# A three-stage kernel in fp32 products on one core: a weight quad's splits and sums spread over its products in the second MoE

## The chip, the cores and the metric

The kernel runs on one core of one Trainium2 chip. The metric is the time of one execution on the device in microseconds (us), here the median of three runs. The core has five engines with a queue of instructions each, which they work off in order: PE (TensorE, matrix products into PSUM), DVE (VectorE), ACT (ScalarE), POOL (GpSimd) and SP, which here only issues DMA transfers. An engine that waits for another's result holds everything behind it in its own queue.

## The reference

Three stages follow each other on 2304 tokens of width 512: a linear attention, a first MoE layer and a second one. Only the second MoE is touched:

```python
def _moe2_ref(x, domain_probs, w1, w2) -> np.ndarray:
    N, D = x.shape                                  # 2304, 512
    E = w1.shape[0]                                 # 4 experts, w1: 4 x 512 x 1024, w2: 4 x 1024 x 512
    p = domain_probs / (domain_probs.sum(-1, keepdims=True) + 1e-09)
    out = np.zeros((N, D), dtype=np.float32)
    for e in range(E):
        h = np.maximum(x @ w1[e], 0.0)
        out += p[:, e:e + 1] * (h @ w2[e])
    return out.astype(np.float32)
```

All experts are computed for all tokens. The result must be good to about fp32, so each factor of a product is split into a rounded high part and the remainder, its low part, and a product is three matmuls (`split3`, line 357: high by high, high by low, low by high).

## The kernel before

The attention and the first MoE (lines 1 to 880, the first 697 us) are recorded into a planner that sets the order of their instructions from costs and due times. The second MoE is written out by hand, in the order in which its instructions stand in the code: 3 passes over 768 tokens each, and in each pass 16 **quads**. A quad is a block of 256 hidden columns of one expert; the program goes through 48 of them (`for q in range(NALL)`, here numbered 0 to 47).

**Layer 1 of a quad** is a fast 2x2 block product: seven products of 384 tokens by 128 columns (`product(1)` to `product(7)`, 6 matmuls each) in place of eight. Their PSUM results are combined on DVE by `plus` (line 975) in a chain of four buffers `cp, cu, cv, cw` (tiles `xc`); ACT copies the first product to `cp` (line 977). Four results of the chain are hidden blocks: `hidden` lets ACT write the high part (relu, line 971) and DVE the low part (line 972). The seven products go through six PSUM banks (`l1b`), so PE can run most of a quad ahead of DVE.

**Layer 2** runs one pair of quads behind: in quad q the pair n2 = q // 2 - 1 is summed over for three blocks of 128 tokens, the **token sums** `l2(0)`, `l2(1)`, `l2(2)` (`layer2`, 12 matmuls of 512 columns each). They alternate between two banks (`l2b`), which DVE empties into the accumulators `yacc` (line 929 the first time in a pass, line 931 later). So `l2(2)` can't begin until DVE has emptied `l2(0)`. PE's order in a quad is product 1, 2, `l2(0)`, product 6, 7, `l2(1)`, product 5, 4, `l2(2)`, product 3. On PE the operands tell them apart: products 1, 2, 6, 7, 5, 4, 3 read `xo0, xo1, xo4, xo5, xo3, xo2, xo6`, and token sums read hidden tiles `h00h` and so on.

**Preparing weights.** Two kinds of weights come through a ring of three staging buffers `raw` (512 KB a load), issued by `load_next` on SP in the fixed order w2 of quad 0, w2 of 1, w1 of 2, w2 of 2, w1 of 3, ... (line 903 issues w1, line 905 w2).
- `w1_steps(q + 1)`, a list `todo` of twelve steps in quad q for the next quad's layer 1: steps 0 to 3 are the sums and differences of weight blocks on DVE (line 800, into two buffers `wtmp`, each of two halves), steps 4 to 7 the high parts on ACT (line 802), steps 8 to 11 the low parts on POOL (line 804). Steps 4, 5, 8 and 9 read `raw` itself, the others the sums.
- `todo2`, the split of the quad's own w2, two halves: ACT high, POOL low (line 948). The token sums of the quad behind an odd one need it first.

**Where they stand before**: `prep(4)` issues the four sums right behind the first `hidden`, ahead of DVE's emptying of `l2(0)`; the ACT steps and the POOL steps come in pairs between later products; `todo2` stands at the end of the quad, and behind it two `load_next`, of which the first brings the w1 that the next quad's `prep(4)` needs. A load's transfer waits until the readers of its staging buffer have finished.

**Special quads.** Behind quads 3 and 19 `x_load` issues eight transfers of the next pass's tokens on SP (line 845), and four differences of them on DVE (`x_diff`, line 851) wait for these. In quads 15 and 31 (`xnew`) ACT and DVE or POOL split the next pass's seven operands (`x_hi`, `x_lo`, lines 859 and 863). In quad 47 there are no w1 steps. Behind it six token sums of the last pair follow.

Of the kernel before, what the change touches and what calls it, by code (L numbers as in the profile page):

```python
# [178 lines left out]
def attention_moe_moe_kernel(  # L179
# [17 lines left out]
    E, _, F2 = w1.shape  # L197
# [25 lines left out]
    def f32(ap):  # L223
        return ap.bitcast(F32)
# [127 lines left out]
    def split3(ps, pairs, start, stop):  # L352
        n = 0
        for (lh, ll), (rh, rl) in pairs:
            for a, b in ((lh, rh), (lh, rl), (ll, rh)):
                n += 1
                PE.matmul(ps, lhsT=a, rhs=b, start=start and n == 1, stop=stop and n == 3 * len(pairs))  # L357
# [414 lines left out]
    def w1_src(q):  # L772
        e, c = divmod(q % NQ, QPE)
        return w1[e, :, c * 256:(c + 1) * 256].rearrange("(k p) f -> p k f", p=128)

    def w2_src(q):
        e, c = divmod(q % NQ, QPE)
        return w2[e, c * 256:(c + 1) * 256, :].rearrange("(c p) d -> p c d", p=128)

    def w1_set(q):  # L780

        return [slots[2 * (q % 2) + i].rearrange(FULL)[:, 0:7 * 256].rearrange("p (o k f) -> p o k f", o=7, k=2) for i in range(2)]

    def w2_set(q):
        t = slots[4 + q % 4]
        return t[:, 0:2], t[:, 2:4]

    def w1_steps(q, raw, ta, tb):
        r = raw.bitcast(F32).rearrange("p (k f) -> p k f", k=4)
        s12, s34 = (f32(t).rearrange("p (o k f) -> p o k f", o=2, k=2) for t in (ta, tb))  # L790
        a11, a12, a21, a22 = r[:, 0:2, 0:128], r[:, 2:4, 0:128], r[:, 0:2, 128:256], r[:, 2:4, 128:256]
        wh, wl = w1_set(q)
        parts = [
            (wh[:, 0:2].rearrange("p o k f -> p (o k) f"), wl[:, 0:2].rearrange("p o k f -> p (o k) f"), r[:, :, 0:128], 512),
            (wh[:, 2], wl[:, 2], a22, 256),
            (wh[:, 3:5].rearrange("p o k f -> p (o k f)"), wl[:, 3:5].rearrange("p o k f -> p (o k f)"), s12.rearrange("p o k f -> p (o k f)"), 512),
            (wh[:, 5:7].rearrange("p o k f -> p (o k f)"), wl[:, 5:7].rearrange("p o k f -> p (o k f)"), s34.rearrange("p o k f -> p (o k f)"), 512),
        ]
        sums = [(s12[:, 0], a21, a22, ALU.add), (s12[:, 1], s12[:, 0], a11, ALU.subtract), (s34[:, 0], a11, a21, ALU.subtract), (s34[:, 1], a12, s12[:, 1], ALU.subtract)]
        steps = [("DVE", 0.36, lambda o=o, a=a, b=b, op=op: DVE.tensor_tensor(out=o, in0=a, in1=b, op=op)) for o, a, b, op in sums]  # L800
        for h, _, src, n in parts:
            steps.append(("ACT", c_act(n), lambda h=h, src=src: ACT.activation(out=h, in_=src, func=ACTF.Copy)))  # L802
        for h, l, src, n in parts:
            steps.append(("POOL", c_pool(n), lambda h=h, l=l, src=src: POOL.tensor_tensor(out=l, in0=src, in1=f32(h), op=ALU.subtract)))  # L804
        return steps
# [36 lines left out]
    def x_load(ps, kh):  # L842
        st = x_tiles()
        for h, o, j, i, n in x_pieces(ps):
            SP.dma_start(out=st["q"][2 * kh + h][:, :, o:o + n], in_=x2f[j][:, 2 * kh:2 * kh + 2, i:i + n])

    def x_diff(i):
        st = x_tiles()
        (b11, b12, b21, b22), (d2, d3, d4) = st["q"], st["t"]
        o, a, b = ((d3, b22, b12), (b12, b12, b11), (d2, b22, b12), (d4, b21, d2))[i]  # L850
        DVE.tensor_tensor(out=o, in0=a, in1=b, op=ALU.subtract)
# [6 lines left out]
    def x_hi(o):  # L858
        ACT.activation(out=x_tiles()["op"][o][0], in_=x_src(o), func=ACTF.Copy)

    def x_lo(o, eng):
        xh, xl = x_tiles()["op"][o]
        eng.tensor_tensor(out=xl, in0=x_src(o), in1=f32(xh), op=ALU.subtract)
# [34 lines left out]
    def load_next():  # L898
        if want:
            layer, q = want.pop(0)  # L900
            t = raw_ring.take().t
            if layer == 1:
                SP.dma_start(out=t.bitcast(F32).rearrange("p (k f) -> p k f", k=4), in_=w1_src(q))
            else:
                SP.dma_start(out=t.bitcast(F32).rearrange("p (c d) -> p c d", c=2), in_=w2_src(q))
            loads[layer, q] = t

    for _ in range(2):
        load_next()

    def hbuf(q, f, t):

        return hid[t][(2 * q + f) % len(hid[t])]

    def layer2(n, t):

        ps, pc = divmod(n, NQ // 2)
        e = 2 * pc // QPE
        y = l2b[(n * TP + t) % 2]
        half, sl = t // (TP // 2), slice(t % (TP // 2) * 128, (t % (TP // 2) + 1) * 128)  # L920
        for i in range(4):
            q, f = 2 * n + i // 2, i % 2
            hh, hl = hbuf(q, f, half)
            vh, vl = w2_set(q)
            split3(y, [((hh[:, sl], hl[:, sl]), (vh[:, f], vl[:, f]))], i == 0, i == 3)
        tt = ps * TP + t
        pe = pr[:, tt, e:e + 1]
        if pc == 0:
            DVE.tensor_scalar(out=acc[t], in0=y, scalar1=pe, scalar2=None, op0=ALU.mult)
        else:  # L930
            DVE.scalar_tensor_tensor(out=acc[t], in0=y, scalar=pe, in1=acc[t], op0=ALU.mult, op1=ALU.add)  # L931
        if pc == NQ // 2 - 1:
            SP.dma_start(out=out[tt * 128:(tt + 1) * 128, :], in_=acc[t])
# [6 lines left out]
    for q in range(NALL):  # L940
        ps, qi = divmod(q, NQ)
        wh, wl = w1_set(q)
        n2 = q // 2 - 1
        todo = []
        if 2 <= q + 1 < NALL:
            todo = [fn for _, _, fn in w1_steps(q + 1, loads.pop((1, q + 1)), tmp_ring.take().t, tmp_ring.take().t)]
        r2, (vh, vl) = loads.pop((2, q)).bitcast(F32).rearrange("p (c d) -> p c d", c=2), w2_set(q)
        todo2 = [lambda c=c: (ACT.activation(out=vh[:, c], in_=r2[:, c], func=ACTF.Copy), POOL.tensor_tensor(out=vl[:, c], in0=r2[:, c], in1=f32(vh[:, c]), op=ALU.subtract)) for c in range(2)]  # L948
        xnew = qi == NQ - 1 and ps + 1 < NPASS

        def product(p):
            o, x = PROD[p]
            bk = l1b[nprod[0] % len(l1b)][:, 0:NH]
            nprod[0] += 1
            split3(bk, [((wh[:, o, k], wl[:, o, k]), (xop[x][0][:, k], xop[x][1][:, k])) for k in range(2)], True, True)
            if xnew:
                x_hi(x)
                x_lo(x, POOL if p in (2, 7, 4) else DVE)
            return bk

        def prep(n):
            for _ in range(min(n, len(todo))):
                todo.pop(0)()

        def l2(i):
            if n2 >= 0:
                layer2(n2, 3 * (q % 2) + i)

        def hidden(f, t, src):
            hh, hl = hbuf(q, f, t)  # L970
            ACT.activation(out=hh, in_=src, func=ACTF.Relu)
            DVE.scalar_tensor_tensor(out=hl, in0=src, scalar=0.0, in1=f32(hh), op0=ALU.max, op1=ALU.subtract)

        def plus(o, bk, a):
            DVE.tensor_tensor(out=o, in0=bk, in1=a, op=ALU.add)  # L975

        ACT.activation(out=cp, in_=product(1), func=ACTF.Copy)  # L977
        p2 = product(2)
        plus(cw, p2, cp)
        hidden(0, 0, cw)  # L980
        prep(4)
        l2(0)
        plus(cu, product(6), cp)
        prep(2)
        plus(cv, product(7), cu)
        prep(2)
        l2(1)
        p5 = product(5)
        plus(cw, p5, cv)
        hidden(1, 1, cw)  # L990
        plus(cu, p5, cu)
        prep(2)
        plus(cv, product(4), cv)
        hidden(1, 0, cv)
        prep(2)
        l2(2)
        plus(cu, product(3), cu)
        hidden(0, 1, cu)
        for fn in todo2:
            fn()  # L1000
        load_next()
        load_next()
        if qi == 3 and ps + 1 < NPASS:
            for kh in range(2):
                x_load(ps + 1, kh)
            for i in range(4):
                x_diff(i)
# [32 lines left out]
```

## Time and profile before

| | |
|---|---|
| median of 3 runs | 1600.21 us (1594.75 to 1601.03) |
| the profiled execution | 1601.69 us |
| its span, first to last instruction | 1599.9 us |
| second MoE, from its first product (695.88 us) to the end | 904 us |
| quads 3 to 47 (738.92 to 1575.67 us) | 836.75 us, 18.6 us each |
| PE busy over the span | 1461.1 us (91%) |

The profile is one execution, with the start and duration of each instruction, the idle time of its engine ahead of it and what ended that idle time (in square brackets). The profile's busy time of PE counts matmuls that overlap in the pipeline, so what a product costs is read from the distance between the starts of two groups, not from the duration of one matmul. PEclk is the share of the full TensorE clock (2.4 GHz) that was granted; 0.5 is the lower of the two levels (1.2 GHz).

### The profile page before, as it was taken

The numbers are of one execution on the slowest core, as the hardware profiler recorded it, in microseconds if no ns is written. First come the engines' busy times: TensorE is split into PE (matmuls) and PEld (weight loads), VectorE is DVE, ScalarE is ACT, GpSimd is POOL, SyncE is SP. The second block draws the span as 40 slices with busy tenths as digits, with TensorE's granted clock in tenths as the row PEclk, the third lists the DMA queues.
The fourth block names the chain that finished last, engine by engine and source line by source line (L and its number), as shares of the span: only waits on it lengthen the run. The fifth ranks groups of instructions, "written<-read, shape, count | busy, mean of one in ns | idle before, by whom it ended". The sixth has DMA issues, their size and how long they took to land.

```text
span 1599.9 us, 24278 instructions
## 1 busy us (share of the span) xinstructions
PE 1461.1 (91%) x9088; PEld 1301.1 (81%) x9088; DVE 1055.0 (66%) x1923; ACT 693.6 (43%) x1639; POOL 684.2 (43%) x587
## 2 busy tenths in 40 slices
PE   8898999999999999989689997988899989999898
PEld 6578988988999999987577776877787877878787
DVE  6787688887666676666566656646666566665663
ACT  5665667666565564443223324323333333332321
POOL 3575446553135244254343435424434444343441
PEclk9989999999999999999899999998999999999999
DMA  6432244433144332121211121221111122112111
GB/s 170 138 91 67 78 134 140 134 113 96 49 148 144 118 115 100 49 69 53 92 54 53 56 77 53 92 92 53 53 53 53 66 84 75 53 53 79 54 53 40
DMA packets 118341, 133.79 MB, mean 84 GB/s; under 512 B 49232, under 2 KB 90320, under 8 KB 118224
## 3 DMA queue, kind: packets, MB, share of 16 engines
q1 hardware_dynamic: 118064, 132.18, 25.2%
q8 instruction: 71, 1.16, 0.3%
q14 instruction: 46, 0.38, 0.1%
q10 hardware_dynamic: 160, 0.07, 0.0%
HBM read 104.44 MB, written 27.79 MB: 83 GB/s over the span
## 4 chain that ended last, share of the span: by engine, by line
PE 34%; DVE 33%; DMA 11%; POOL 8%; ACT 8%; issue 5%; SPq 1%; DVEq 0%; POOLq 0%; ACTq 0%
PE bank L357 12%; PE acc L357 11%; DMA raw<-in_moe_w_dram 10%; DVE xc L975 9%; DVE wtmp L800 8%; POOL wslot L948 7%; PE bank L583 3%; DVE yacc L931 3%; PE bank L483 2%; ACT wslot L948 2%; DVE hs L636 2%; DVE th L638 1%; PE bank L567 1%; PE bank L541 1%; PE bank L433 1%
## 5 line engine op out<-in xcount | busy, mean ns | idle before, releaser
L357 PE MATMUL acc<-gh,wslot 128*128 128x288 f32 x1024 | 245.1, 306 | 2.5 <-ACT gh L639 2.5
L948 POOL TENSOR_TENSOR wslot<-raw,wslot 128x512 fp32r<-128x512 f32 x96 | 123.2, 1306 | 286.9 <-ACT wslot L948 286.9
L804 POOL TENSOR_TENSOR wslot<-raw,wslot 128x512 fp32r<-128x512 f32 x96 | 108.0, 1146 | 217.8 <-ACT wslot L802 213.1
L237 POOL TENSOR_TENSOR gl<-th,gh 128x288 fp32r<-128x288 f32 x112 | 98.4, 879 | 217.9 <-ACT gh L639 161.1
L800 DVE TENSOR_TENSOR wtmp<-raw 128x256 f32<-128x256 f32 x96 | 88.2, 918 | 147.0 <-DMA raw<-in_moe_w_dram 147.0
L357 PEld LDWEIGHTS acc<-gh,wslot 128*128 128x128 f32 x1024 | 176.4, 190 | 7.6 <-issue 4.1
L357 PE MATMUL acc<-gl,wslot 128*128 128x288 f32 x512 | 152.0, 297 | 0.8 <-POOL gl L237 0.8
L804 POOL TENSOR_TENSOR wslot<-wtmp,wslot 128x512 fp32r<-128x512 f32 x96 | 131.7, 1392 | 1.5 <-ACT wslot L802 1.5
L802 ACT ACTIVATE wslot<-raw 128x512 fp32r<-128x512 f32 x96 | 45.1, 516 | 185.8 <-DMA raw<-in_moe_w_dram 185.8
L357 PE MATMUL bank<-xt0h,wslot 128*128 128x288 f32 x512 | 117.0, 304 | 6.5 <-DVE u L589 2.5
L638 DVE COPY_PREDICATED th<-sq,hs 128x288 f32<-128x288 int32 x128 | 79.7, 624 | 59.1 <-ACT sq L637 58.8
L357 PE MATMUL bank<-xt1h,wslot 128*128 128x288 f32 x512 | 116.3, 302 | 2.4 <-DVE qm L570 2.4
L637 ACT ACTIVATE sq<-sq,b_m 128x288 f32<-128x288 f32 x128 | 68.9, 540 | 111.2 <-DVE hs L636 110.3
L975 DVE TENSOR_TENSOR xc<-bank,xc 128x384 f32<-128x384 f32 x168 | 91.0, 550 | 21.5 <-ACT xc L977 18.9
L975 DVE TENSOR_TENSOR xc<-acc,xc 128x384 f32<-128x384 f32 x168 | 91.1, 550 | 21.4 <-ACT xc L977 18.0
L634 DVE SCALAR_TENSOR_TENSOR hs<-bank,sq 128x288 f32<-128x288 f32 x128 | 57.9, 453 | 61.9 <-ACT th L633 61.3
L357 PEld LDWEIGHTS acc<-gl,wslot 128*128 128x128 f32 x512 | 97.6, 191 | 1.0 <-POOL gl L237 1.0
L357 PEld LDWEIGHTS bank<-xt0h,wslot 128*128 128x128 f32 x512 | 87.7, 193 | 8.8 <-DVE u L589 2.6
L802 ACT ACTIVATE wslot<-wtmp 128x512 fp32r<-128x512 f32 x96 | 60.4, 631 | 78.6 <-DVE wtmp L800 75.9
L357 PEld LDWEIGHTS bank<-xt1h,wslot 128*128 128x128 f32 x512 | 87.4, 192 | 3.5 <-DVE qm L570 2.9
L636 DVE SCALAR_TENSOR_TENSOR hs<-sq,hs 128x288 f32<-128x288 f32 x128 | 84.7, 662 | 0.0
L357 PE MATMUL bank<-xt0l,wslot 128*128 128x288 f32 x256 | 76.8, 300 | 0.0
(336 smaller groups left out, 4127.5 us busy)
## 6 DMA issues: line engine op xcount, KB each, us to landing
raw<-in_moe_w_dram SPq DMA_DIRECT2D x96, 512.0 KB, 4.3
raw<-in_moe_w_in_dram SPq DMA_DIRECT2D x16, 512.0 KB, 4.3
raw<-in_moe_w_out_dram SPq DMA_DIRECT2D x16, 512.0 KB, 4.5
qraw<-in_q_dram SPq DMA_DIRECT2D x32, 144.0 KB, 2.8
x2s<-x2p SPq DMA_DIRECT2D x8, 576.0 KB, 3.0
x2p<-x2s SPq DMA_DIRECT2D x8, 576.0 KB, 3.8
x2f<-x2p SPq DMA_DIRECT2D x8, 576.0 KB, 2.8
out_dram<-yacc SPq DMA_DIRECT2D x18, 256.0 KB, 2.0
```

Of the source, the lines that this page charges most:

```text
L237: return add("POOL", c_pool(n), lambda: POOL.tensor_tensor(out=o, in0=a, in1=b, op=op), deps, due, bufs)
L357: PE.matmul(ps, lhsT=a, rhs=b, start=start and n == 1, stop=stop and n == 3 * len(pairs))
L583: PE.matmul(side(ab)[:, e, r], lhsT=x.t[:, e, r * QP:(r + 1) * QP], rhs=kv.t[:, e, ab], start=True, stop=True)
L634: y1 = add("DVE", c_dve(N), lambda: DVE.scalar_tensor_tensor(out=hs.t, in0=at(bk)[:, 0:N], scalar=P1, in1=sq.t, op0=ALU.mult, op1=ALU.mult ...
L636: y3 = add("DVE", c_dve(N), lambda: DVE.scalar_tensor_tensor(out=hs.t, in0=sq.t, scalar=P0 / P1, in1=hs.t, op0=ALU.add, op1=ALU.mult), [y1 ...
L637: x3 = add("ACT", c_act(N, ptr=True), lambda: ACT.activation(out=sq.t, in_=sq.t, func=ACTF.Relu, scale=-1.0, bias=b_m[:, 0:1]), [y3], due ...
L638: y4 = add("DVE", c_dve(N), lambda: DVE.copy_predicated(out=th.t, mask=sq.t.bitcast(I32), data=hs.t), [x3, y2, y3], due + 1.4, [th, sq, hs])
L800: steps = [("DVE", 0.36, lambda o=o, a=a, b=b, op=op: DVE.tensor_tensor(out=o, in0=a, in1=b, op=op)) for o, a, b, op in sums]
L802: steps.append(("ACT", c_act(n), lambda h=h, src=src: ACT.activation(out=h, in_=src, func=ACTF.Copy)))
L804: steps.append(("POOL", c_pool(n), lambda h=h, l=l, src=src: POOL.tensor_tensor(out=l, in0=src, in1=f32(h), op=ALU.subtract)))
L948: todo2 = [lambda c=c: (ACT.activation(out=vh[:, c], in_=r2[:, c], func=ACTF.Copy), POOL.tensor_tensor(out=vl[:, c], in0=r2[:, c], in1=f32 ...
L975: DVE.tensor_tensor(out=o, in0=bk, in1=a, op=ALU.add)
```

## The change

In the second MoE's loop the same instructions are issued in another order; nothing is added or left out.
- Three loads are issued ahead of the loop, not two.
- `prep` takes the numbers of the steps to issue.
- The two halves of `todo2` move from the end of the quad to its beginning: the first behind the copy of product 1, the second behind `l2(0)`. Behind the second one stands a `load_next`, whose staging buffer the split has just read.
- The first two sums of `w1_steps` stand behind the `plus` of product 6, the other two behind the last `plus` of product 5. So DVE's emptying of `l2(0)` stands ahead of all sums, and that of `l2(1)` ahead of the second two.
- The ACT and POOL steps follow in pairs: 4 and 8 behind product 6, 5 and 9 behind `l2(1)`, 6 and 10 behind product 5, 7 and 11 behind `l2(2)`.
- At the end of the quad one `load_next` is left, whose staging buffer the w1 steps have just read; `x_load` and `x_diff` follow it as before.

```diff
-    for _ in range(2):
+    for _ in range(3):
         load_next()
...
-        def prep(n):
-            for _ in range(min(n, len(todo))):
-                todo.pop(0)()
+        def prep(*which):
+            for i in which:
+                if todo:
+                    todo[i]()
...
         ACT.activation(out=cp, in_=product(1), func=ACTF.Copy)
-        p2 = product(2)
-        plus(cw, p2, cp)
+        todo2[0]()
+        plus(cw, product(2), cp)
         hidden(0, 0, cw)
-        prep(4)
         l2(0)
+        todo2[1]()
+        load_next()
         plus(cu, product(6), cp)
-        prep(2)
+        prep(0, 1, 4, 8)
         plus(cv, product(7), cu)
-        prep(2)
         l2(1)
+        prep(5, 9)
         p5 = product(5)
         plus(cw, p5, cv)
         hidden(1, 1, cw)
         plus(cu, p5, cu)
-        prep(2)
+        prep(2, 3, 6, 10)
         plus(cv, product(4), cv)
         hidden(1, 0, cv)
-        prep(2)
         l2(2)
+        prep(7, 11)
         plus(cu, product(3), cu)
         hidden(0, 1, cu)
-        for fn in todo2:
-            fn()
-        load_next()
-        load_next()
+        if todo:
+            load_next()
```

The lines below `prep` move by one or two numbers: line 971 becomes 972, 972 becomes 973, 975 becomes 976, 977 becomes 979. On DVE, from the first `plus` of a quad to the emptying of its third token sum, before (`wtmp` is the sums, `yacc` the emptying of a token sum):

```order
L975 TENSOR_TENSOR xc_6283<-bank_84,xc_6280 128x384
L972 SCALAR_TENSOR_TENSOR h04l<-xc_6283,h04h 128x384
L800 TENSOR_TENSOR wtmp_135<-raw_132 128x256
L800 TENSOR_TENSOR wtmp_135<-wtmp_135,raw_132 128x256
L800 TENSOR_TENSOR wtmp_136<-raw_132 128x256
L800 TENSOR_TENSOR wtmp_136<-raw_132,wtmp_135 128x256
L931 SCALAR_TENSOR_TENSOR yacc_7559<-acc_83,pr,yacc_7559 128x512
L975 TENSOR_TENSOR xc_6281<-bank_85,xc_6280 128x384
L975 TENSOR_TENSOR xc_6282<-bank_86,xc_6281 128x384
L931 SCALAR_TENSOR_TENSOR yacc_7560<-bank_87,pr,yacc_7560 128x512
```

The same stretch of DVE now:

```order
L976 TENSOR_TENSOR xc_6283<-bank_84,xc_6280 128x384
L973 SCALAR_TENSOR_TENSOR h04l<-xc_6283,h04h 128x384
L931 SCALAR_TENSOR_TENSOR yacc_7559<-acc_83,pr,yacc_7559 128x512
L976 TENSOR_TENSOR xc_6281<-bank_85,xc_6280 128x384
L800 TENSOR_TENSOR wtmp_135<-raw_132 128x256
L800 TENSOR_TENSOR wtmp_135<-wtmp_135,raw_132 128x256
L976 TENSOR_TENSOR xc_6282<-bank_86,xc_6281 128x384
L931 SCALAR_TENSOR_TENSOR yacc_7560<-bank_87,pr,yacc_7560 128x512
```

The emptying of the first token sum no longer stands behind the four sums. On ACT, one quad and the head of the next before (`wslot<-raw 128x512 x2` of line 948 is the w2 split, `xc` the copy of product 1, `h..h` the relu):

```order
L977 ACTIVATE xc_6280<-bank_86 128x384
L971 ACTIVATE h04h<-xc_6283 128x384
L802 ACTIVATE wslot_126<-raw_132 128x512
L802 ACTIVATE wslot_126<-raw_132 128x256
L802 ACTIVATE wslot_126<-wtmp_135 128x512
L802 ACTIVATE wslot_126<-wtmp_136 128x512
L971 ACTIVATE h15h<-xc_6283 128x384
L971 ACTIVATE h05h<-xc_6282 128x384
L971 ACTIVATE h14h<-xc_6281 128x384
L948 ACTIVATE wslot_130<-raw_134 128x512 x2
L977 ACTIVATE xc_6280<-acc_80 128x384
```

The same quad on ACT now:

```order
L979 ACTIVATE xc_6280<-bank_86 128x384
L948 ACTIVATE wslot_130<-raw_134 128x512
L972 ACTIVATE h04h<-xc_6283 128x384
L948 ACTIVATE wslot_130<-raw_134 128x512
L802 ACTIVATE wslot_126<-raw_132 128x512
L802 ACTIVATE wslot_126<-raw_132 128x256
L972 ACTIVATE h15h<-xc_6283 128x384
L802 ACTIVATE wslot_126<-wtmp_135 128x512
L972 ACTIVATE h05h<-xc_6282 128x384
L802 ACTIVATE wslot_126<-wtmp_136 128x512
L972 ACTIVATE h14h<-xc_6281 128x384
L979 ACTIVATE xc_6280<-acc_80 128x384
```

The w2 split has gone from the end of the quad to its head, on either side of the first relu, and nothing stands any more between the last relu and the next quad's copy. On POOL the two instructions of the w2 split stand ahead of the quad's four w1 steps, where they stood behind them. PE's order is the same.

## Rows read from the trace of the kernel before

**Rows 1.** Busy time by stretch: the stretch in us from the span's start, its length, then for each engine its busy time and in brackets its instructions, PEclk, DMA share and GB/s. The rows are quads 3 to 47 together; a stretch of the first MoE; quad 47, which has no w1 steps; and the first token sum behind the wait of quad 4.

```profile
738.92:1575.67 836.75, 744.30 (x3512) 643.59 (x3511) 514.68 (x823) 264.89 (x505) 346.02 (x272) 0.96 0.19 63
...
500.00:600.00 100.00, 100.00 (x754) 100.00 (x753) 67.97 (x147) 54.89 (x132) 36.18 (x37) 1.00 0.36 123
...
1560.03:1575.67 15.64, 15.64 (x80) 14.11 (x79) 9.91 (x17) 4.05 (x8) 2.54 (x2) 1.00 0.01 2
...
781.60:785.92 4.32, 4.32 (x13) 3.43 (x14) 3.58 (x7) 0.54 (x3) 1.66 (x2) 0.64 0.00 0
```

**Rows 2.** What PE's matmuls waited for from 697 to 1600 us: waiting engine and line, whom it waited for, total us, times, longest.

```profile
PE bank L357 <- DVE yacc L931: 30.4, 6, 12.8
PE acc L357 <- DVE yacc L931: 28.1, 19, 2.6
PE bank L357 <- POOL wslot L948: 20.7, 39, 0.9
PE bank L357 <- ACT wslot L948: 12.2, 5, 4.9
```

**Rows 3.** PE in order of time, quads 40 and 41: start, duration, operation, count and idle time. Kept are the first matmul of product 6, of `l2(1)` and of product 5 of quad 40, and that of `l2(2)` of quad 41.

```profile
1440.50 0.33 PE L357 MATMUL bank<-xo4h,wslot 128*128 128x384 f32 x1
...
1442.58 0.63 PE L357 MATMUL acc<-wslot,h04h 128*128 128x512 f32 x2
...
1445.34 0.33 PE L357 MATMUL bank<-xo3h,wslot 128*128 128x384 f32 x1
...
1465.03 0.73 PE L357 MATMUL acc<-wslot,h14h 128*128 128x512 f32 x2 [1.77 <-DVE yacc L931]
```

**Rows 4.** DVE in order of time, from the first `plus` of quad 37 to that of quad 38 (that of quad 38 is the last row); left out are the rows between the emptying of `l2(0)` and the end of the quad.

```profile
1385.04 0.56 DVE L975 TENSOR_TENSOR xc<-bank,xc 128x384 f32<-128x384 f32 x1 [0.86 <-ACT xc L977]
1386.19 0.95 DVE L972 SCALAR_TENSOR_TENSOR h02l<-xc,h02h 128x384 fp32r<-128x384 f32 x1 [0.59 <-ACT h02h L971]
1390.30 0.42 DVE L800 TENSOR_TENSOR wtmp<-raw 128x256 f32<-128x256 f32 x1 [3.16 <-DMA raw<-in_moe_w_dram]
1390.76 0.43 DVE L800 TENSOR_TENSOR wtmp<-wtmp,raw 128x256 f32<-128x256 f32 x1
1391.10 1.52 DVE L800 TENSOR_TENSOR wtmp<-raw 128x256 f32<-128x256 f32 x1
1392.54 0.94 DVE L800 TENSOR_TENSOR wtmp<-raw,wtmp 128x256 f32<-128x256 f32 x1
1393.40 0.74 DVE L931 SCALAR_TENSOR_TENSOR yacc<-acc,pr,yacc 128x512 f32<-128x512 f32 x1
...
1402.76 0.56 DVE L975 TENSOR_TENSOR xc<-acc,xc 128x384 f32<-128x384 f32 x1 [0.86 <-ACT xc L977]
```

**Rows 5.** POOL over the same stretch: the w2 split of quad 36, then the four w1 steps of quad 37.

```profile
1384.19 2.54 POOL L948 TENSOR_TENSOR wslot<-raw,wslot 128x512 fp32r<-128x512 f32 x2 [6.01 <-ACT wslot L948]
1390.97 2.23 POOL L804 TENSOR_TENSOR wslot<-raw,wslot 128x512 fp32r<-128x512 f32 x2 [4.24 <-ACT wslot L802]
1393.16 2.72 POOL L804 TENSOR_TENSOR wslot<-wtmp,wslot 128x512 fp32r<-128x512 f32 x2
```

**Rows 6.** SP over the same stretch: the first of the two loads issued there, the w1 load.

```profile
1386.75 0.37 SPq L903 DMA_DIRECT2D raw<-in_moe_w_dram  x1
```

**Rows 7.** The token load behind quad 3, SP's rows: one w1 load, one w2 load, eight transfers of tokens.

```profile
761.12 0.37 SPq L903 DMA_DIRECT2D raw<-in_moe_w_dram  x1
761.58 0.46 SPq L905 DMA_DIRECT2D raw<-in_moe_w_dram  x1
762.09 4.91 SPq L845 DMA_DIRECT2D xq<-x2f  x8
```

**Rows 8.** DVE behind that token load: the first of the four differences, the first `plus` of quad 4, the first sum, and the emptying of `l2(0)`.

```profile
772.39 0.96 DVE L851 TENSOR_TENSOR xd<-xq,xq 128x768 f32<-128x768 f32 x1 [13.82 <-DMA xq<-x2f]
...
776.25 0.55 DVE L975 TENSOR_TENSOR xc<-acc,xc 128x384 f32<-128x384 f32 x1
...
777.86 0.42 DVE L800 TENSOR_TENSOR wtmp<-raw 128x256 f32<-128x256 f32 x1
...
780.80 0.74 DVE L931 SCALAR_TENSOR_TENSOR yacc<-bank,pr,yacc 128x512 f32<-128x512 f32 x1
```

**Rows 9.** PE's longest waits: `l2(2)` of quads 4 and 20, behind the two token loads.

```profile
781.60 1.22 PE L357 MATMUL bank<-wslot,h04h 128*128 128x512 f32 x2 [12.75 <-DVE yacc L931]
...
1085.50 1.22 PE L357 MATMUL bank<-wslot,h00h 128*128 128x512 f32 x2 [11.07 <-DVE yacc L931]
```

**Rows 10.** PE in `l2(0)` of quad 2, the first token sum of the stage: the wait for the w2 split, and the first matmul of product 6 behind it.

```profile
722.84 0.51 PE L357 MATMUL bank<-wslot,h02h 128*128 128x512 f32 x1 [2.02 <-ACT wslot L948]
...
726.49 0.52 PE L357 MATMUL acc<-xo4h,wslot 128*128 128x384 f32 x1
```

**Rows 11.** PE behind quad 47: the first matmul of the first three token sums of the last pair.

```profile
1575.67 0.63 PE L357 MATMUL bank<-wslot,h02h 128*128 128x512 f32 x2
...
1581.16 1.05 PE L357 MATMUL acc<-wslot,h02h 128*128 128x512 f32 x2
...
1585.00 0.62 PE L357 MATMUL bank<-wslot,h02h 128*128 128x512 f32 x2
```

**Rows 12.** DVE in quad 15: the two operand splits of the next pass that took least and most.

```profile
972.21 0.96 DVE L863 TENSOR_TENSOR xo0l<-xq,xo0h 128x768 fp32r<-128x768 f32 x1 [1.22 <-ACT xo0h L859]
...
980.09 2.23 DVE L863 TENSOR_TENSOR xo4l<-xd,xo4h 128x768 fp32r<-128x768 f32 x1
```

## The prediction

> **What bounds the kernel now.** I read the busy time by stretch first. Quads 3 to 47 take 836.75 us, 18.6 us each, and PEclk there is 0.96; in the first MoE PE is busy without a gap at full clock [rows 1]. So the second MoE is where time can be won, and the question is what a quad would take if PE never waited. The timeline of PE gives it: two products take 1442.58 - 1440.50 = 2.08 us, 1.04 each, and a token sum 1445.34 - 1442.58 = 2.76 us [rows 3]. Seven and three of them make 7 x 1.04 + 3 x 2.76 = 15.56 us. Quad 47, which prepares no weights, shows it whole: 15.64 us [rows 1]. I take 15.6. Three us of each quad are waiting and what follows from it.
>
> PE's waits name two causes: the emptying of a token sum by DVE, and the w2 split by ACT and POOL [rows 2]. DVE's timeline shows why it is late. It stands 3.16 us for a load of weights ahead of the sums, and the emptying of `l2(0)` stands behind the sums [rows 4]. That load went out at 1386.75 [rows 6], right behind the w2 split, which POOL ended at 1386.73 [rows 5]. The split stands at the end of the quad, behind the relu that waits for DVE. So this is a loop: DVE's chain, w2 split, load, landing, sums, DVE's chain. It closes in 1402.76 - 1385.04 = 17.72 us [rows 4] and PE follows it. Odd quads lose time ahead of `l2(2)` (1.77 us in quad 41 [rows 3]), even ones inside `l2(0)`, where w2 of the quad before isn't split yet.
>
> **The change part by part.**
>
> *The loop is opened.* The w1 load now goes out in the first third of a quad and is read in the next quad's second third, some 15 us later; before, DVE met it 3.5 us behind its issue (1386.75 to 1390.30 [rows 4, 6]). The w2 load has a quad more still. The w2 split is done about 10 us ahead of the end of its quad. The emptying of `l2(0)` stands ahead of all sums. What is late next? Two candidates: PE itself, and DVE's chain without the load.
>
> DVE's chain in quad 37 is 17.72 us. Without the load's 3.16 and without the 0.86 for ACT's copy, which stood behind the w2 split and now stands right behind the last relu, 13.70 remain [rows 4]. In it are operations that took longer than their kind: a sum takes 0.42, but two took 1.52 and 0.94 while POOL worked on its w1 steps, and the low part of the first hidden block took 0.95 rather than 0.56 while POOL split w2 [rows 4, 5]. That is 1.10 + 0.52 + 0.39 = 2.01 us, so the bare chain is 11.69. With POOL's six instructions spread, more of these eight operations can meet one. I place them by the order: the first low part meets the first half of the w2 split (about 0.4), the first two sums meet steps 8 and 9 (up to 1.6, as now), the second two meet step 10 (about 1.0), the last low part hardly meets step 11 (0.1). That is 3.1, and the chain 14.8 us, below 15.6. PE is the bound, with 0.8 us to spare. The other moved instructions are under this cover: ACT is busy for 265 of 837 us and POOL for 346 [rows 1]. On ACT a half of the w2 split (0.6) stands between the copy and the relu, but the relu must wait for a `plus` of 0.55 on DVE anyway. SP's new load in mid-quad waits for POOL's second half, and behind it only outputs and the next load are queued. If DVE's cover fails, see the second rival.
>
> So quads 3 to 47 go from 836.75 to 45 x 15.6 = 702.0 us: **-134.8**, before the special quads are paid for again.
>
> *The two token loads.* In quads 4 and 20 PE waits 12.75 and 11.07 us [rows 9], because DVE stands for the tokens and only then gets to `l2(0)`. `x_diff` stays where it is, so a wait remains. In time of quad 4: PE reaches `l2(2)` after 6 products and 2 token sums, 6 x 1.04 + 2 x 2.76 = 11.8 us. The load ahead of `x_load` now waits for step 11. Product 4 ends 3.8 us ahead of the quad's end; a `plus` (0.55), a relu (0.6), step 7 (0.6) and step 11 (2.72 / 2 = 1.4 [rows 5]) follow it, with up to 2.5 us of sums that are held up. So SP gets on between -0.7 and 2; I take 1.5. From SP's first load to DVE's release 772.39 - 761.12 = 11.27 us pass [rows 7, 8], of which one load of two falls away; its issue is 0.46, and at most a third of the bytes, so 0.5 to 2: I take 1.5. Release at 1.5 + 9.8 = 11.3. From release to PE's restart 781.60 - 772.39 = 9.21 us pass [rows 8, 9], but 780.80 - 777.86 = 2.94 of them are the sums, which no longer stand there: 6.3. PE restarts at 17.6 and has waited 5.8 us, against 12.75. Behind such a wait the clock is down: a token sum took 4.32 rather than 2.76 us at PEclk 0.64 [rows 1]. With 1.6 for that and 0.6 for w1 steps that come late in the next quad (0 to 1), a token load costs 8 us, two **+16** (bounds 10 and 24).
>
> *The two quads with operand splits.* DVE gets four splits of 0.96 to 2.23 us [rows 12], some 5.5, which 0.8 us a quad can't hide; but PE may run ahead of DVE until the next quad's `l2(0)` needs the third hidden block, about 4 us. I take 0.75 each, **+1.5** (0 to 6).
>
> *The beginning.* In quad 2 PE waited in `l2(0)` 2.02 us and more for the w2 split and reached product 6 at 726.49 [rows 10]. The hidden blocks of quad 1 are then the last to be ready, and w2 no longer. I take **-5** (between the wait alone, -2, and -6, which adds the copies that stood behind the w2 split in quads 0 and 1).
>
> *The end.* The first two token sums of the last pair took 5.49 and 3.84 us [rows 11] instead of 2.76, for the same split and the clock behind it: **-3.8**.
>
> Sum on the profiled execution: 1601.7 - 134.8 - 5 - 3.8 + 16 + 1.5 = 1475.6 us. Its span is 1599.9, so 1.8 us lie around it and stay. The median of the runs is 1600.2, 0.1% below the profiled execution; I don't correct for it. **Forecast: 1476 us**, with bounds of the terms together 1462 to 1495.
>
> **Rivals.**
>
> *DVE becomes the bound.* If POOL's spread instructions hold up DVE not for 3.1 but for 4.5 to 5 us a quad, the chain is 16.2 to 16.7 and PE waits again: 45 x 0.6 to 1.1 = 27 to 50 us, 1503 to 1526. For it: only three operations met POOL before and cost 2.0 us [rows 4, 5]. Against it: operations that read PSUM, the `plus` and the emptying, kept their 0.55 and 0.74 us beside POOL, and they are most of the chain.
>
> *POOL holds up DVE with all it has (slower).* A sum that met POOL ended about when POOL's instruction did [rows 4, 5]. If each us of POOL's 2.54 + 2.23 + 2.72 = 7.5 a quad were lost to DVE, the chain would be 11.69 + 7.5 = 19.2 us and the time 1601.7 + 45 x 19.2 - 836.75 - 8.8 = 1620. It is slower than before from 7.1 us a quad on. Against it: DVE has eight such operations in 15.6 us, and half of POOL's time now falls where DVE reads PSUM.
>
> The Trainium skill ("SBUF — State Buffer", section "SBUF: two separate sides") speaks for this rival: VectorE and GpSimd share a pair of ports as a lock, and an instruction of VectorE with two SBUF inputs and one of GpSimd keep each other out for the whole of the one that began first. The sum of 1.52 us, begun 0.13 us behind a POOL instruction, agrees with it; by the rule without a look at where the eight fall, the slower rival would be the forecast.
>
> *The change doesn't do what it says:* the loads are issued earlier in the code but not in time, since SP is held by something else (an output's transfer, the token load), and the loop of 17.72 us stays. Then only the w2 waits at both ends go: 1601.7 - 8.8 = 1593, and at most a few us less. Against it: the only other things in SP's queue are 18 outputs and 16 token transfers in 904 us.
>
> **How the numbers follow.** Forecast 0.79, DVE as the bound 0.14, loop kept 0.04, slower 0.03. The range takes all of the forecast's bounds and the near half of the first rival, and a little below for terms that I sized too high: 1460 to 1515. About 0.5% is what a measurement of this kernel tells from no change. Faster by more: forecast, first rival and half of the third, 0.95; within 0.5%: 0.02; slower: 0.03.
>
> **What would show it.** Right: quads of 15.6 to 15.7 us by the starts of `xo0h` on PE; no idle time of DVE ahead of line 800 for a DMA, and none of PE for line 948; two waits of 5 to 8 us left on PE, both ahead of `l2(2)` and behind line 851; PEclk 0.99 or more outside them. Wrong: PE waiting for line 931 in each quad with DVE busy all through and sums of 1 us and more (first rival); line 800 or 948 still waiting for `raw` (loop kept). My weakest terms are the two token loads and how often DVE's sums meet POOL.

## The result and the profile after

| | before | after |
|---|---|---|
| median | 1598.8 us (1594.75 to 1601.03, 4 runs) | 1467.12 us (1466.11 to 1468.74, 4 runs) |
| the profiled execution | 1601.69 us | 1467.26 us |
| quads 3 to 47 | 836.75 us | 710.70 us |
| behind quad 47 | 24.23 us | 20.38 us |

The median before is now that of four runs, one more than ahead of the prediction. The ratio is 0.918, with a 95% interval of 0.9158 to 0.9202. Of the 134.4 us between the two profiled executions 126.05 come from quads 3 to 47, 3.85 from the six token sums behind them, and 4.5 from the beginning: quad 3 starts at 734.40 rather than 738.92 us.

Busy time by stretch after the change, columns as in [rows 1]: quads 3 to 47, quad 37, quad 4 and quad 20 (behind the token loads), and what follows quad 47.

```profile
734.40:1445.10 710.70, 706.60 (x3512) 635.72 (x3512) 536.14 (x826) 252.28 (x507) 354.71 (x273) 1.00 0.23 74
1273.06:1288.70 15.64, 15.64 (x80) 14.11 (x80) 11.62 (x18) 5.40 (x12) 7.60 (x6) 1.00 0.24 69
750.04:767.63 17.59, 15.94 (x79) 14.07 (x79) 11.67 (x17) 3.85 (x9) 6.20 (x5) 1.00 0.47 150
1002.56:1022.50 19.94, 17.49 (x80) 15.21 (x80) 12.70 (x20) 4.85 (x10) 6.66 (x6) 0.91 0.42 133
1445.10:1465.48 20.38, 16.52 (x73) 13.32 (x72) 5.62 (x8) 0.53 (x1) 0.00 (x0) 0.97 0.20 77
```

Quad 37 with all its weight steps now takes what quad 47 took without them [rows 1]: 15.64 us, PE without a gap. From quad 3 on all but four quads take 15.64 us. Quads 4 and 20 take 1.95 and 4.30 us more, and quads 16 and 32, behind the operand splits, 0.33 each.

PE's waits in the second MoE, columns as in [rows 2]:

```profile
PE bank L357 <- DVE yacc L931: 4.1, 2, 2.5
PE bank L357 <- POOL wslot L804: 1.9, 1, 1.9
PE bank L357 <- DVE xc L976: 1.8, 1, 1.8
PE bank L357 <- ACT wslot L802: 0.8, 1, 0.8
PE acc L357 <- DVE xc L976: 0.6, 1, 0.6
```

The 91 us of [rows 2] have become 9. The first row is the two token loads; the other four are single waits of quads 1 and 2. The waits for the w2 split (line 948) are gone.

DVE in quad 37, rows that answer to [rows 4]: the low part of the first hidden block, the emptying of `l2(0)`, the `plus` of product 6, the first two sums, the emptying of `l2(1)`, the second two sums.

```profile
1276.97 1.04 DVE L973 SCALAR_TENSOR_TENSOR h02l<-xc,h02h 128x384 fp32r<-128x384 f32 x1 [0.59 <-ACT h02h L972]
1278.10 0.75 DVE L931 SCALAR_TENSOR_TENSOR yacc<-acc,pr,yacc 128x512 f32<-128x512 f32 x1
1279.16 0.56 DVE L976 TENSOR_TENSOR xc<-acc,xc 128x384 f32<-128x384 f32 x1 [0.31 <-PE acc L357]
1279.63 1.07 DVE L800 TENSOR_TENSOR wtmp<-raw 128x256 f32<-128x256 f32 x1
1280.74 0.85 DVE L800 TENSOR_TENSOR wtmp<-wtmp,raw 128x256 f32<-128x256 f32 x1
...
1282.96 0.75 DVE L931 SCALAR_TENSOR_TENSOR yacc<-bank,pr,yacc 128x512 f32<-128x512 f32 x1 [0.91 <-PE bank L357]
...
1286.12 1.20 DVE L800 TENSOR_TENSOR wtmp<-raw 128x256 f32<-128x256 f32 x1
1287.24 0.41 DVE L800 TENSOR_TENSOR wtmp<-raw,wtmp 128x256 f32<-128x256 f32 x1
```

The 3.16 us for a DMA are gone, and what is in brackets now is PE: DVE waits for it, 1.53 us in the quad (0.31 and 0.91 here, and 0.31 at 1284.03). Three of the four sums and the first low part still run long beside POOL.

POOL's w2 split of quad 37, then SP's two loads of that quad:

```profile
1276.30 2.87 POOL L948 TENSOR_TENSOR wslot<-raw,wslot 128x512 fp32r<-128x512 f32 x2 [1.36 <-ACT wslot L948]
```

```profile
1279.20 0.37 SPq L903 DMA_DIRECT2D raw<-in_moe_w_dram  x1
1287.72 0.37 SPq L905 DMA_DIRECT2D raw<-in_moe_w_dram  x1
```

Each load goes out as the last reader of its buffer ends: the w1 load 0.03 us behind the w2 split (1276.30 + 2.87 = 1279.17), the w2 load 0.07 us behind the fourth sum (1287.24 + 0.41 = 1287.65). The w1 load is read by the next quad's sums at 1295.3, 16 us later.

### The profile page after: what moved, and what is told of

Read it like the earlier page. It is cut to its first block, busy times and chain, and to the rows that moved or that the text cites. A ratio compares the mean times of both kernels' runs of the same rounds, so it can differ in the third digit from the quotient of the medians.

```text
span 1465.5 us, 24201 instructions
## 1 busy us (share of the span) xinstructions
PE 1419.0 (97%) x9088; PEld 1290.3 (88%) x9088; DVE 1075.5 (73%) x1923; ACT 679.7 (46%) x1639; POOL 692.8 (47%) x587
## 4 chain that ended last, share of the span: by engine, by line
PE 82%; DVE 10%; ACT 3%; issue 1%; POOL 1%; DMA 1%; SPq 1%; ACTq 0%; DVEq 0%; POOLq 0%
PE bank L357 35%; PE acc L357 35%; PE bank L583 4%; PE bank L483 2%; DVE hs L636 2%; DVE th L638 1%; PE bank L567 1%; PE bank L541 1%; PE bank L433 1%; DVE hs L634 1%; DVE wtmp L308 1%; DVE wtmp L307 1%; DVE th L635 1%; ACT sq L637 1%; SPq L245 1%
## 5 line engine op out<-in xcount | busy, mean ns | idle before, releaser
L804 POOL TENSOR_TENSOR wslot<-wtmp,wslot 128x512 fp32r<-128x512 f32 x96 | 124.4, 1297 | 270.1 <-ACT wslot L802 167.7
L948 POOL TENSOR_TENSOR wslot<-raw,wslot 128x512 fp32r<-128x512 f32 x96 | 137.9, 1457 | 94.7 <-ACT wslot L948 94.7
L804 POOL TENSOR_TENSOR wslot<-raw,wslot 128x512 fp32r<-128x512 f32 x96 | 108.7, 1152 | 0.0
L800 DVE TENSOR_TENSOR wtmp<-raw 128x256 f32<-128x256 f32 x96 | 98.3, 1024 | 0.0
L632 ACT ACTIVATE sq<-bank 128x288 f32<-128x288 f32 x128 | 52.4, 409 | 55.5 <-PE bank L357 54.2
L357 PE MATMUL bank<-xt1l,wslot 128*128 128x288 f32 x256 | 76.6, 299 | 0.0
```

Of the source, the lines that this page charges most:

```text
L632: x1 = add("ACT", c_act(N, True), lambda: ACT.activation(out=sq.t, in_=at(bk)[:, 0:N], func=ACTF.Square), [a], due, [sq], frees=[bk])
```

## The experiments

Each run's time is a median, and its ratio is to runs of the kernel before on the same chip. The length of a quad is the distance between the starts of `xo0h` on PE in its trace.

**Loads at their old place.**

```diff
-    for _ in range(3):
+    for _ in range(2):
         load_next()
...
         todo2[1]()
-        load_next()
...
-        if todo:
-            load_next()
+        load_next()
+        load_next()
```

> The change with its loads put back: two loads ahead of the loop, both next loads issued at a quad's end; splits and sums stay where the change put them. My theory now: the place of a load in the code does nothing, since SP comes to it early and stands there until the buffer's last reader is done; what opened the loop is that the w2 split, the last reader, stands at the quad's head. Then quads of 15.64 us and 1467 us (1464 to 1471) as with the change. Rival, the reading in the prediction (the w1 load had to be issued in the first third of a quad): the load is met by DVE again at 1 to 3.5 us of waiting a quad, of which 1.5 are hidden; up to 45 x 2 = 90 us more, 1475 to 1557.

Measured: 1468.28 us, ratio 0.9176 (0.9142 to 0.921), the same as the change. Its busy time for quads 3 to 47, then SP's loads in one quad:

```profile
735.40:1446.02 710.62, 706.68 (x3512) 635.78 (x3512) 536.25 (x826) 253.22 (x507) 354.20 (x273) 1.00 0.23 74
```

```profile
1241.68 0.37 SPq L905 DMA_DIRECT2D raw<-in_moe_w_dram  x1
1248.79 0.37 SPq L903 DMA_DIRECT2D raw<-in_moe_w_dram  x1
1257.33 0.37 SPq L905 DMA_DIRECT2D raw<-in_moe_w_dram  x1
```

The loads still stand 7.1 and 8.5 us apart, as in the change (1272.10, 1279.20, 1287.72). SP's queue holds little else, so SP stands at a load long before the buffer is free, wherever the code issues it. So this part of the change, the loads issued earlier, costs and brings nothing where the w2 split stands at the head.

**The w2 split alone at the head**: w1's steps at their places of before.

```diff
         hidden(0, 0, cw)
+        prep(0, 1, 2, 3)
         l2(0)
         todo2[1]()
         load_next()
         plus(cu, product(6), cp)
-        prep(0, 1, 4, 8)
+        prep(4, 5)
         plus(cv, product(7), cu)
+        prep(6, 7)
         l2(1)
-        prep(5, 9)
...
-        prep(2, 3, 6, 10)
+        prep(8, 9)
         plus(cv, product(4), cv)
         hidden(1, 0, cv)
+        prep(10, 11)
         l2(2)
-        prep(7, 11)
```

> The change with w1's sums, copies and low parts put back to their places of before (four sums behind the first hidden block, ahead of the first token sum's emptying); the w2 split at the quad's head and the loads stay. My theory: the w2 split alone opens the loop; a quad stays at 15.64 us or a little over, 1467 to 1480. Rival: the emptying of the first token sum must stand ahead of the sums; if DVE's four sums (0.4 to 1.5 us each, 3 us together) delay it, PE waits up to 1 us a quad, 1485 to 1515. The two token loads would cost up to 3 us more each, since the sums stand behind them again.

Measured: 1467.27 us, ratio 0.9162 (0.9127 to 0.9198). Quads 3 to 47:

```profile
728.90:1438.98 710.08, 704.82 (x3511) 634.79 (x3511) 559.86 (x825) 264.84 (x506) 363.26 (x272) 1.00 0.23 73
```

710.08 us, as with the whole change. DVE is busy for 24 us more, and PE doesn't notice. Moving the w2 split is enough; neither the spread sums nor the early emptying of `l2(0)` is needed for the time. The loads stand here where the change put them, and the w2 split alone with the loads at their old place was not run. Nor does a run separate the two things that the moved split does: it frees the load's buffer early, and it has w2 ready early.

**The spread of w1's steps alone**: the w2 split and both loads at the quad's end, and two loads ahead of the loop.

```diff
-    for _ in range(3):
+    for _ in range(2):
         load_next()
...
-        todo2[0]()
...
-        todo2[1]()
-        load_next()
...
-        if todo:
-            load_next()
+        for fn in todo2:
+            fn()
+        load_next()
+        load_next()
```

> The change with only its spread of w1's steps; the w2 split and both loads stand at the quad's end as before, two loads ahead of the loop. My theory: the loop of split, load and sums stays, but shorter, since fewer operations of DVE lie between the sums and the last relu: first sums to last relu some 10.2 us, split 3.2, load 3.5, together 16.9 us a quad, so 1467 + 45 x 1.3 = 1525 (1510 to 1550). Rival (the spread of the sums is what counts): 15.64 us a quad and 1467 to 1475.

Measured: 1540.85 us, ratio 0.9617 (0.9581 to 0.9654). Two neighbouring quads; then what PE waited for in the second MoE, and DVE's first row of waits for quads 3 to 47:

```profile
1385.47:1402.29 16.82, 16.20 (x79) 13.95 (x79) 10.63 (x18) 5.51 (x12) 7.16 (x6) 1.00 0.19 63
1402.29:1417.93 15.64, 15.64 (x79) 14.11 (x79) 10.28 (x18) 5.20 (x11) 7.21 (x6) 1.00 0.20 67
```

```profile
PE bank L357 <- ACT wslot L948: 19.1, 8, 5.8
PE bank L357 <- POOL wslot L948: 18.9, 45, 0.9
PE bank L357 <- DVE yacc L931: 18.2, 2, 9.5
```

```profile
DVE wtmp L800 <- DMA raw<-in_moe_w_dram: 57.8, 33, 3.8
```

The time lies within my range, but not by the mechanism that I expected. DVE does meet its load again (57.8 us), but in the steady quads this doesn't put off the quad's end. ACT's last relu of the quad that ends at 1385.47 shows it:

```profile
1387.20 0.53 ACT L972 ACTIVATE h16h<-xc 128x384 fp32r<-128x384 f32 x1 [1.23 <-DVE xc L976]
```

It begins 1387.20 - 1385.47 = 1.73 us behind the next quad's start, as in the change (1274.80 - 1273.06 = 1.74 us). So the loop of split, load and sums doesn't set the time of these quads. What PE waits for is the w2 split itself (line 948), inside `l2(0)`, and it costs 1.2 us in every second quad. Most of what is lost beyond that is in the special quads: 12.8 us more in each of quads 4 and 20, 9.1 and 9.7 in 16 and 32. So the spread is worth 836.75 - 777.4 = 59 us where the w2 split stays late, and nothing where it stands early.

**The tokens' differences two quads later.**

```diff
         if qi == 3 and ps + 1 < NPASS:
             for kh in range(2):
                 x_load(ps + 1, kh)
+        if qi == 5 and ps + 1 < NPASS:
             for i in range(4):
                 x_diff(i)
```

> The change with the four differences of the tokens moved from the end of the fourth quad of a pass to the end of the sixth; the token loads stay where they are. My theory: in quads 5 and 21 DVE stands 4.5 and 5.3 us for the token transfers, which puts off the first token sum's emptying and costs PE 1.95 + 4.30 = 6.25 us; two quads later the transfers have long landed, so the waits go: 1461 (1459 to 1463). Rival: the cost is not DVE's wait but the transfers' share of SP and the load of weights behind them; then 1467 stays.

Measured: 1461.92 us, ratio 0.9141 (0.9112 to 0.917), 5.2 us below the change. The expectation counts quads from 1: its quads 5 and 21 are 4 and 20 here. All that PE waits for in the second MoE:

```profile
PE bank L357 <- POOL wslot L804: 2.0, 1, 2.0
PE bank L357 <- DVE xc L976: 1.8, 1, 1.8
```

Quads 4 and 20 take 15.64 us, and the second MoE from its first product to the end 763.1 us rather than 769.4. What a token load costs is DVE's standing for it, not the transfers.

**Copies added on DVE**: two, five and eight a quad.

```diff
+        for _ in range(5):
+            DVE.tensor_copy(out=spare, in_=p5)
         prep(2, 3, 6, 10)
```

> The change with two copies of a product's PSUM bank to a spare tile added to DVE in each quad of the second MoE, ahead of the third sum (the output doesn't change). A measure of DVE's spare time. My theory: with the change PE is the bound and DVE waits 1.5 us a quad for it; two copies of some 0.5 us are 1.0 us and vanish: 1467 to 1470. Rival (DVE has the 0.8 us to spare that the prediction worked out, or less): 0.2 us a quad or more come through, 1476 and up.

> The same with five copies a quad, 2.4 us of DVE's time. By 1.5 us to spare, 0.9 us a quad come through, 45 x 0.9 = 40: 1507 (1495 to 1515). By the prediction's 0.8 us to spare it is 1.6 us a quad, 1539. If DVE had no part in the bound at all, 1467.

> The change with eight copies of a product's PSUM bank a quad on DVE, 8 x 0.57 = 4.6 us. With five of them (2.85 us) the steady quads stayed at 15.64 us, with DVE without a wait for PE. My theory: that used up DVE's spare time, so what is more comes through whole: 15.6 + 3 x 0.57 = 17.3 us a quad, 45 x 1.7 = 76 us, and some 30 in the special quads, 1573 (1550 to 1590). Rival (DVE gives still more time back, as its operations slide away from POOL's): under 16.5 us a quad, below 1535.

Measured: 1471.86 us (ratio 0.9217, 0.9194 to 0.9241), 1494.0 (0.9364, 0.9336 to 0.9393) and 1577.22 (0.987, 0.9843 to 0.9896). With two and with five the steady quads stay at 15.64 us. So the expectation for five, 0.9 us in each quad, was wrong: what five copies cost lies in quads 1, 2, 4 to 6, 16, 20 and 32. The time with two lies between what I expected and the rival. In its profile, an execution of 1467.7 us, the second MoE takes only 0.7 us longer than in the change; where the rest of the median's 4.7 us lies is not shown. DVE with five copies, from one quad's copies to the next's:

```profile
1280.87 2.92 DVE L997 COPY spare<-acc 128x384 f32<-128x384 f32 x5
1283.70 0.41 DVE L800 TENSOR_TENSOR wtmp<-raw 128x256 f32<-128x256 f32 x1
1284.04 0.42 DVE L800 TENSOR_TENSOR wtmp<-raw,wtmp 128x256 f32<-128x256 f32 x1
...
1289.41 1.03 DVE L974 SCALAR_TENSOR_TENSOR h00l<-xc,h00h 128x384 fp32r<-128x384 f32 x1 [0.59 <-ACT h00h L973]
...
1291.49 0.41 DVE L800 TENSOR_TENSOR wtmp<-raw 128x256 f32<-128x256 f32 x1
1291.93 1.40 DVE L800 TENSOR_TENSOR wtmp<-wtmp,raw 128x256 f32<-128x256 f32 x1
...
1296.45 2.91 DVE L997 COPY spare<-acc 128x384 f32<-128x384 f32 x5
```

DVE's round is 1296.45 - 1280.87 = 15.58 us, without a wait for PE. The copies take 1283.70 - 1280.87 = 2.83 of them, so DVE's own chain is 12.75 us. Without its waits for PE it was 15.64 - 1.53 = 14.11 us in quad 37 of the change, so the chain gave up 1.36 us. Some 0.9 of them came because its operations slid away from POOL's: the second two sums are back at 0.41 and 0.42, and what POOL adds to DVE's operations (the stretch) is 0.47 + 0.98 = 1.45 us rather than some 2.3. Most of the other 0.5 are in the gaps between DVE's instructions. With eight copies DVE is the bound; the row is two quads:

```profile
1382.53:1417.26 34.73, 32.24 (x158) 27.96 (x157) 29.45 (x53) 10.79 (x22) 15.55 (x13) 1.00 0.18 61
```

17.37 us a quad, against 15.58 + 3 x 0.57 = 17.3 worked out ahead. DVE's spare time under the change is thus 15.64 - 12.75 = 2.9 us a quad.

**POOL's w1 steps twice, and left out.**

```diff
             for i in which:
                 if todo:
                     todo[i]()
+                    if i >= 8:
+                        todo[i]()
```

> The change with each of POOL's four low parts of w1 issued twice in the second MoE (the second writes the same values): POOL's 7.6 us a quad become 12.8. It tries the prediction's second and third rivals: POOL holds up DVE's operations that have two inputs in SBUF. My theory: they meet POOL about twice as often, the 2.4 us by which DVE's operations are stretched become 4 to 5, and of that 1.5 are hidden: 0.1 to 1.1 us a quad come through, 1472 to 1517. Rival (a stretch of the sums never reaches PE): 1467 to 1470. Rival (each us of POOL is lost to DVE): 5.2 - 1.5 = 3.7 us a quad, 1634.

Measured: 1490.03 us, ratio 0.9341 (0.9318 to 0.9363). The row is four steady quads, 62.56 = 4 x 15.64 us; PE's waits from 745 us on follow:

```profile
1284.25:1346.81 62.56, 62.56 (x314) 56.45 (x313) 51.61 (x74) 21.58 (x44) 49.39 (x40) 1.00 0.20 68
```

```profile
PE bank L357 <- DVE yacc L931: 6.6, 2, 3.4
PE bank L357 <- POOL wslot L804: 6.1, 4, 4.3
PE acc L357 <- POOL wslot L804: 4.6, 2, 4.3
```

POOL is busy for 12.3 us a quad and DVE for 12.9, and PE has no gap: of the 0.1 to 1.1 us a quad that I expected nothing came, so it is by luck that the time lies in my range. The 23 us lie where POOL itself becomes the bound, behind the operand splits (quads 16 and 32: 23.35 and 22.85 us, waiting for line 804), in quads 4, 5, 20 and 21, and at the beginning.

```diff
             for i in which:
-                if todo:
+                if todo and (i < 8 or q < 2):
                     todo[i]()
```

> The change with POOL's four low parts of w1 left out from the third quad of the second MoE on (the low parts of older weights stand in their place). POOL has 2.5 us a quad left instead of 7.6. My theory: POOL is what stretches DVE's sums, so they all take 0.42 us instead of up to 1.2, and PE doesn't notice, since DVE's time isn't the bound: quads of 15.64, 1460 to 1467 (less only at the beginning and in the quads with operand splits). Rival (the sums' length is DVE's own, from the tiles): they stay at 1.0 us and more.

Measured: 1466.05 us, ratio 0.9176 (0.9153 to 0.92). DVE's sums from 1270 to 1425 us, by shape: busy us and mean ns, without POOL's steps, and in the change itself:

```profile
L800 DVE TENSOR_TENSOR wtmp<-raw 128x256 f32<-128x256 f32 x20 | 8.3, 414 | 0.0
L800 DVE TENSOR_TENSOR wtmp<-wtmp,raw 128x256 f32<-128x256 f32 x10 | 4.2, 425 | 0.3
```

```profile
L800 DVE TENSOR_TENSOR wtmp<-raw 128x256 f32<-128x256 f32 x20 | 22.6, 1131 | 0.0
...
L800 DVE TENSOR_TENSOR wtmp<-wtmp,raw 128x256 f32<-128x256 f32 x10 | 8.5, 849 | 0.3
```

The steady quads stay at 15.64 us. POOL is what stretches the sums, 1131 ns against 414, and the time doesn't depend on it. That POOL stretches them agrees with the rule of the Trainium skill that the prediction weighed ("SBUF — State Buffer", section "SBUF: two separate sides").

**Two versions of the beginning**, on top of the late differences. The domain probabilities are loaded at the kernel's start; the first quad's w2 split stands at its end. The second version also lets quad 1 issue its twelve w1 steps behind its first hidden block, ahead of the `plus` of product 6, and split w2 behind product 5; each moved split takes its `load_next` along. In the first version that load stays in mid-quad: the first quad's split reads its staging buffer after a later load was issued into it, so that quad's second layer is computed with other weights. The lines are those of the second version.

```diff
+    ACT.dma_start(out=pr, in_=probs.rearrange("(t p) e -> p t e", p=128))
...
-        todo2[0]()
+        if q > 1:
+            todo2[0]()
...
+        if q == 1:
+            prep(0, 1, 2, 3, 4, 8, 5, 9, 6, 10, 7, 11)
+            todo = []
```

> The version with the late differences, and two waits of the beginning taken away: the domain probabilities are loaded at the kernel's start (DVE stood 4.4 us for them ahead of the first product's sum), and in the first quad alone the w2 split stands at the end again (ACT stood 5.6 us for its load ahead of the first relu). My theory: of the 5.2 us that PE waits in the second and third quad 3 to 5 go: 1457 (1455 to 1460). Rival: the w1 steps of the next quad are what PE waits for there and they stand behind POOL, so nothing is won: 1461 to 1462.

> The version with the late differences, and the beginning put in order: the domain probabilities are loaded at the kernel's start; the first quad splits its w2 at its end, the second prepares w1 ahead of everything and splits w2 behind its fourth product. My theory: of the 5.2 us that PE waits in the second and third quad some 3 go: from the first product of the second MoE to the end 1460 minus 3, so 1458 in all (1456 to 1461). Rival: the second quad's twelve steps still end too late for the third, and DVE's sums hold up the plus operations: 1462 or more.

Measured: 1462.05 us (ratio 0.916, 0.9139 to 0.9181) and 1459.76 us (0.9139, 0.9117 to 0.9162). In the first version quad 1 no longer waits, but quad 2 waits 3.3 us for a low part of w1, which stands on POOL behind all four halves of the two w2 splits; the rival was right. In the second, which came out in my range, quad 1 takes 7.28 us, and 2.8 us of PE's waits are left in the second MoE. From its first product to the end the second MoE takes 1456.0 - 696.9 = 759.1 us, against 761.3 in the first version, 763.1 with the late differences alone and 769.4 with the change. The medians of the last two versions don't tell them apart.

## Why the prediction held, and where it didn't

| term | predicted | measured |
|---|---|---|
| 45 quads | 702.0 us | 45 x 15.64 = 703.8 |
| two token loads | +16 | 1.95 + 4.30 = +6.25 |
| operand splits | +1.5 | 2 x 0.33 = +0.7 |
| beginning | -5 | -4.5 |
| end | -3.8 | -3.85 |

The forecast of 1476 us lies 9 us above the median, and every rival's time (1503 us and more) lies far from it. The bounds of its terms as they stand add up to 1467.1 to 1491.1, not 1462 to 1495, so the profiled execution (1467.26) is at their lower edge.

**PE as the bound at 15.6 us** was right, and it is nearly all of the gain. It was read from PE's own pace [rows 3] and from quad 47 [rows 1], not from a list of what the change removes, so it held although part of the reason given for it was wrong.

**"The loop is opened"** was right: no wait of DVE for a load of weights, none of PE for line 948. That the w1 load goes out in the first third of a quad was near (6.1 us into it). The w2 load, which was to have a quad more, has only 3 us more: it is read 1306.87 - 1287.72 = 19.2 us behind its issue. But the prediction lets the reader think that the new `load_next` opens the loop. It doesn't: without it the time is the same. The load waits for the w2 split to have read its buffer, and that split moved. Nor was the emptying of `l2(0)` ahead of the sums a part of it, as the run with the w2 split alone shows.

**DVE's chain** was put at 14.8 us with 0.8 to spare; it is 12.75 us when DVE is pressed, with 2.9 to spare. I had placed 3.1 us of stretch (what POOL adds to DVE's operations) as a fixed cost. It is 2.3 while DVE has time (0.48 + 0.65 + 0.42 + 0.78 in quad 37) and 1.45 when it has none, and the bare chain is 12.75 - 1.45 = 11.3 us rather than 11.69. So the first rival was some 3 us a quad away from deciding, and the slower one further: with POOL's steps doubled, PE still ran without a gap.

**The beginning** came near its -5, but from two amounts, of which the prediction had one. Quad 2 took 19.76 rather than 26.17 us, and quad 1 took 11.25 rather than 9.57: ahead of the stage's first relu ACT now stands 5.64 us for the w2 load. In the two versions of the beginning, which move that split back and load the probabilities early, quad 1 takes 7.51 and 7.28 us; which of the two moves brought this was not separated.

**The two token loads** are the term that was mis-sized, by 9.7 us; the sum of the forecast, 1475.6, and the profiled execution differ by 8.3. The first step of it that failed is "the load ahead of `x_load` now waits for step 11". Step 11 reads the sums and not `raw`; the last reader of that buffer is the fourth sum. SP, then DVE's release by the tokens, then PE's restarts, each in quads 4 and 20:

```profile
749.07 0.37 SPq L905 DMA_DIRECT2D raw<-in_moe_w_dram  x1
749.49 4.05 SPq L845 DMA_DIRECT2D xq<-x2f  x8
...
1001.60 0.37 SPq L905 DMA_DIRECT2D raw<-in_moe_w_dram  x1
```

```profile
757.40 0.96 DVE L851 TENSOR_TENSOR xd<-xq,xq 128x768 f32<-128x768 f32 x1 [4.50 <-DMA xq<-x2f]
...
1010.72 0.96 DVE L851 TENSOR_TENSOR xd<-xq,xq 128x768 f32<-128x768 f32 x1 [5.31 <-DMA xq<-x2f]
```

```profile
763.67 0.74 PE L357 MATMUL bank<-wslot,h04h 128*128 128x512 f32 x2 [1.65 <-DVE yacc L931]
...
1016.99 1.15 PE L357 MATMUL bank<-wslot,h00h 128*128 128x512 f32 x2 [2.45 <-DVE yacc L931]
```

SP got on 1.0 us ahead of quad 4 (750.04 - 749.07), not 1.5 behind its start; from there to the release 757.40 - 749.07 = 8.3 us passed, not 9.8. The last step held: 763.67 - 757.40 = 6.27 against 6.3. PE then waited 1.65 us, not 5.8. In quad 20 the load went out 1.0 us ahead as well (1002.56 - 1001.60), the release came 1010.72 - 1001.60 = 9.1 us behind it, and PE waited 2.45 us. So of the 9.7 us the wrong name cost 2.5 at each token load, about half. The time from that load to the release was put 1.5 and 0.7 us too long, and the fall of the clock that I had charged to both came in quad 20 alone.

## What to carry to other kernels

When a load comes too late, look first for what still reads the staging buffer that it is to fill, and move that reader; moving the load itself in a queue that already stands waiting for the buffer does nothing. Forecast the time from the pace of the engine that will be left as the bound, and find how far the next engine is from it by adding known work to it: the idle time that a profile shows was a lower end here (1.53 us against 2.9), since operations that were held up by a neighbour shrank when they slid. For every wait of a moved instruction, read in the code which operands its last reader really takes; one wrong name cost about half of the largest error here.

## What the runs showed that I had not expected

- DVE took in 2.83 us of copies a quad where it showed 1.53 us of waiting: its sums beside POOL went from 1.20 to 0.41 us as they slid behind POOL's instructions.
- TensorE's clock behind a wait: the two stretches from PE's restart to the end of the token sum,

```profile
1016.99:1021.46 4.47, 4.47 (x13) 3.53 (x14) 3.84 (x7) 0.62 (x3) 2.86 (x3) 0.62 0.41 121
763.67:766.60 2.93, 2.93 (x13) 2.39 (x14) 2.90 (x5) 0.04 (x1) 2.89 (x3) 1.00 0.35 112
```

  Behind the wait of 2.45 us most of the stretch ran at the lower level (PEclk 0.62), and it cost 1.7 us; behind that of 1.65 us the clock stayed full.
- The time ahead of the second MoE, where all these kernels but the two last versions issue the same instructions, differed between their profiles: its first product started at 696.1 us in the change, at 689.0 in the run with the w2 split alone and at 701.0 with POOL's steps doubled. So differences of a few us are read from the second MoE alone. What sets the difference stays open.
